# Stores, loads and buffers moved around the seams of a fused attention and two-MoE kernel

## The chip, the cores and the metric

The kernel runs on one core of a Trainium2 chip. TensorE multiplies matrices into PSUM banks; ScalarE, VectorE and GpSimd work on the results in SBUF; SyncE issues the DMA transfers, one after the other, and each of its instructions waits for what it needs before the next one is looked at. The metric is the device time of one execution in microseconds; lower is better. In the profile PE, ACT, DVE, POOL and SP are TensorE, ScalarE, VectorE, GpSimd and SyncE.

## What is computed

Attention of 4 x 8 heads over 576 tokens of width 64, its local part mixed with a read from a memory, then two gated layers over all 2304 tokens of width 512 with a hidden width of 1536. The weight matrices come as float64 words; the kernel turns them into float32 itself.

```python
def _attn_ref(q, k, v, M_prev, z_prev, beta):
    scores = scale * np.matmul(q, k.transpose(0, 1, 3, 2))
    ...
    local = np.matmul(a, v)
    ...
    return (g * mem_out + (1 - g) * local).astype(np.float32)

def _moe_ref(x, w_gate, w_val, w_out):
    gate = 1.0 / (1.0 + np.exp(-(x @ w_gate)))
    val = x @ w_val
    return (gate * val @ w_out).astype(np.float32)

def _moe2_ref(x, w_gate, w_val, w_out):
    g = x @ w_gate
    silu = g * (1.0 / (1.0 + np.exp(-g)))
    val = x @ w_val
    return (silu * val @ w_out).astype(np.float32)
```

## The kernel before

Every operand of a matmul is split into a rounded high part and a low rest, and a product is three passes (high x high, high x low, low x high). The program runs through six stretches.

*Attention* (to about 366 us). Its order is made by due times in a table. Beside it, part of the first layer's weights is converted from words, and values `x @ w_val` for the first tokens are computed ahead and stored to DRAM (`vs`).

*Last values* (`values`, 367 to 392 us). Twelve chunks of 12 matmuls for 384 tokens. ScalarE copies each bank to a buffer `vo`, of which there are two, and SyncE stores it to `vs`. At the same time `right(j)` prepares token block j = 0 and 2 for the blocks: it loads rows `xraw` of `xs` (four tiles, two for each half k), builds seven sums on VectorE and casts them on ScalarE to `xop`. Up to here a scheduler sets the order.

*First blocks* (`blocks`, 392 to 581 us). From here on the order is as written. A weight matrix is cut in six groups p of 256 hidden columns; a run (s, j) multiplies group p of the gate (s = 0) or value matrix (s = 1) with token block j (2 x 384 tokens) by seven products instead of eight, each of six matmuls (L828). In group 0 the runs are run 0 = (0, 0), run 1 = (0, 2), run 2 = (1, 2), run 3 = (0, 1); later groups have (0, 0), (0, 1), (0, 2), (1, 2), so run 5 is (0, 1) of group 1. Only for j = 2 are values computed; for j = 0 and 1 they are known and are loaded from `vs` (`vi`, two tiles of a run, in four buffers). Each product has a number n, seven for a run; the work behind a product is put down for a later number (`later`) and done in `slot(n)`: `keep` copies a bank to c (ScalarE, L874), `add` adds a bank to c (VectorE, L877), `finish` makes one of four quarters of h (ScalarE L837, VectorE L839 or L841). When both quarters of a half f are done, `finish` has SyncE store that half to `hs` (L845) at once: halves f = 1 and f = 0 of a run that starts at n are complete in slots n + 10 and n + 13. h tiles are taken two at a time when a run with s = 0 begins, from five buffers (six in the second layer). Other work is put into slots by `put(at, steps, first, last)`: `right(1)` (rows loaded in slots 0 and 13, used from slots 6 and 15), the seven weight operands of the next half group (`kept` loads the kept weights `ws` into a `raw` buffer, two of which exist; for group 1's values in slot 31, used from slot 37), and conversions of output weights.

*First down projection* (`outputs(0)`, 582 to 738 us). 72 steps (t, m): four or three matmul chains of one tile t of 384 tokens with chunk m of the hidden width, 12 matmuls (L974). `hidden` loads a tile of `hs` to `hd`, casts it on ScalarE (L956) and subtracts on VectorE (L957), two steps ahead; `pairs[i]` loads two chunks of converted output weights into a `raw` buffer and splits them, `words` loads and converts the last two chunks from their words. The result `yb` stays in SBUF, the last third goes to `xs` in DRAM.

*Second blocks* (740 to 1002 us) and *second down projection* (`outputs(1)`, to the end) do the same for the second layer with Silu, six runs in a group and no known values. In both layers the first four loads of `hd` (`prelude`) stand in the last slots of the blocks; in the second layer they take c buffers, each of which comes free with the last operation on its c.

## Time and profile before

| | us |
|---|---|
| three runs | 1150.32, 1154.95, 1156.98 |
| median | 1154.95 |
| the profiled execution, own time | 1159.61 |
| its span, first to last instruction | 1157.8 |
| PE busy / DVE busy / ACT busy | 1111.7 / 805.5 / 599.9 |

Busy time is an average over the six stretches. In the blocks and down projections TensorE runs on end and rarely stops, so each stop is read by itself: the timeline of PE shows it in brackets with its length and the instruction that ended it, and the timelines of the other engines show what that instruction waited for. The granted clock (PEclk) is a share of 2.4 GHz.

### The profile page before, as it was taken

Reading aid. Unit: us, or ns where it says so; the run is one execution under the profiler, and the core shown is the slowest. Engines: PE = TensorE matmul, PEld = TensorE weight load, DVE = VectorE, ACT = ScalarE, POOL = GpSimd, SP = SyncE. Lnnn points to the kernel's source line nnn. Section 1 sums busy time; section 2 is a strip of 40 time slices with the busy share of each in tenths; the row PEclk is TensorE's granted clock in tenths of the full one; section 3 lists DMA queues with packets and bytes.
Section 4 is the critical chain, followed back from the end, with each engine's and each line's share of the span. In section 5 each row is a group of like instructions: output and inputs, shape, how many; then the busy total and the mean of one; then the engine's idle time right before and its main releaser. Section 6 shows DMA issues by size and latency. Waiting matters only on the chain.

```text
span 1157.8 us, 19120 instructions
## 1 busy us (share of the span) xinstructions
PE 1111.7 (96%) x6416; PEld 1004.8 (87%) x6416; DVE 805.5 (70%) x2020; ACT 599.9 (52%) x1470; POOL 164.2 (14%) x209
## 2 busy tenths in 40 slices
PE   7899999998999888999999999999999999899998
PEld 5577877776877888999989999999999999788887
DVE  7898868678767777788865644687877877553332
ACT  5666765575567755555544433555445445332222
POOL 3675542344331000000000000000000000000000
PEclk9888999799799999999999999999999999999999
DMA  5566537445411556666775333334444443554443
GB/s 135 173 185 178 157 98 221 118 128 168 150 55 56 191 173 209 224 223 226 241 239 163 93 95 108 104 107 130 143 147 120 154 134 131 183 168 126 126 123 103
DMA packets 162356, 173.77 MB, mean 150 GB/s; under 512 B 69329, under 2 KB 127697, under 8 KB 162257
## 3 DMA queue, kind: packets, MB, share of 16 engines
q1 hardware_dynamic: 162112, 172.54, 48.3%
q8 instruction: 51, 0.84, 0.3%
q14 instruction: 49, 0.39, 0.1%
q10 hardware_dynamic: 144, 0.00, 0.0%
HBM read 112.20 MB, written 60.29 MB: 149 GB/s over the span
## 4 chain that ended last, share of the span: by engine, by line
PE 76%; DMA 6%; DVE 5%; ACT 2%; issue 1%; SPq 0%; ACTq 0%; DVEq 0%
PE ps L828 34%; PE ps L971 13%; PE ps L974 11%; PE gv L742 6%; PE sc L316 3%; PE av L396 3%; DMA xraw<-xs 2%; PE tp L363 2%; PE sc L302 1%; DMA hd<-hs 1%; PE av L387 1%; DMA raw<-ws 1%; DMA raw<-in_moe_w_gate_dram 1%; PE tp L254 1%; PE tp L355 1%
## 5 line engine op out<-in xcount | busy, mean ns | idle before, releaser
L828 PE MATMUL ps<-xop,wset 128*128 128x384 f32 x2520 | 445.6, 337 | 12.3 <-ACT c L874 12.3
L828 PEld LDWEIGHTS ps<-xop,wset 128*128 128x128 f32 x2520 | 441.2, 188 | 15.7 <-ACT c L874 15.5
L957 DVE TENSOR_TENSOR hl<-hd,hl 128x384 fp32r<-128x384 f32 x144 | 80.3, 558 | 151.8 <-ACT hl L956 150.8
L956 ACT CAST hl<-hd 128x384 fp32r<-128x384 f32 x144 | 74.0, 514 | 189.0 <-PE ps L971 84.7
L874 ACT COPY c<-ps 128x384 f32<-128x384 f32 x180 | 86.0, 479 | 116.4 <-PE ps L828 115.5
L742 PE MATMUL gv<-x,w 128*128 128x256 f32 (+2 forms) x720 | 131.3, 327 | 3.5 <-ACT vo L31 1.7
L877 DVE TENSOR_TENSOR c<-ps,c 128x384 f32<-128x384 f32 x180 | 99.6, 554 | 43.6 <-ACT c L874 20.2
L742 PEld LDWEIGHTS gv<-x,w 128*128 128x128 f32 x720 | 112.4, 202 | 13.0 <-issue 6.8
L974 PE MATMUL ps<-hl,xop 128*128 128x384 f32 x648 | 114.0, 336 | 0.0
L974 PEld LDWEIGHTS ps<-hl,xop 128*128 128x128 f32 x648 | 112.6, 188 | 0.0
L971 PE MATMUL ps<-xop,hl 128*128 128x512 f32 x486 | 111.9, 391 | 0.0
L971 PEld LDWEIGHTS ps<-xop,hl 128*128 128x128 f32 x486 | 91.9, 189 | 19.3
L338 POOL TENSOR_SCALAR s<-s,sum,omg 128x512 f32<-128x512 f32 (+2 forms) x92 | 72.5, 799 | 111.1 <-DVE sum L334 19.7
L837 ACT ACTIVATE h<-c 128x384 f32<-128x384 f32 x108 | 56.7, 525 | 58.0 <-DVE c L877 57.8
L330 ACT ACTIVATE s<-s,nm 128x256 f32<-128x256 f32 (+3 forms) x128 | 71.8, 563 | 15.6 <-DVE nm L319 14.5
L316 PE MATMUL sc<-qka 64*128 64x384 f32 (+3 forms) x384 | 74.8, 386 | 4.5 <-DVE nm L319 2.2
L319 DVE CUSTOM_DVE_ANT_0 s<-sc,mask 128x256 f32<-128x256 f32 (+3 forms) x128 | 59.7, 485 | 17.1 <-PE tp L355 8.9
L316 PEld LDWEIGHTS sc<-qka 64*128 64x128 f32 x384 | 48.6, 211 | 20.8 <-issue 5.1
L500 ACT ACTIVATE a<-raw 128x512 f32<-128x512 f32 x72 | 48.4, 673 | 33.7 <-DMA raw<-in_moe_w_gate_dram 19.5
L31 ACT COPY p<-tp 128x512 f32<-128x512 f32 x96 | 45.0, 494 | 25.4 <-PE av L396 12.5
L507 DVE SCALAR_TENSOR_TENSOR a<-raw,a 128x512 int32<-128x512 int32 x72 | 53.3, 740 | 0.2
L511 DVE SCALAR_TENSOR_TENSOR a<-raw,a 128x512 int32<-128x512 int32 x72 | 50.3, 698 | 0.3
(143 smaller groups left out, 1482.9 us busy)
## 6 DMA issues: line engine op xcount, KB each, us to landing
hs<-h SPq DMA_DIRECT2D x72, 384.0 KB, 2.6
hd<-hs SPq DMA_DIRECT2D x144, 192.0 KB, 2.5
raw<-in_moe_w_val_dram SPq DMA_DIRECT2D x24, 512.0 KB, 4.2
raw<-in_moe_w_gate_dram SPq DMA_DIRECT2D x24, 512.0 KB, 4.4
raw<-in_moe_w_out_dram SPq DMA_DIRECT2D x24, 512.0 KB, 3.9
ws<-a SPq DMA_DIRECT2D x44, 256.0 KB, 2.4
vi<-vs SPq DMA_DIRECT2D x24, 384.0 KB, 4.2
xraw<-xs SPq DMA_DIRECT2D x16, 384.0 KB, 3.9
```

The costliest lines, as they stand in the source:

```text
L316: nc.tensor.matmul(o, lhsT=qk[hr, x, 0, qs], rhs=qk[hr, y, 1, 0:n], start=k == 0, stop=k == 2)
L319: nc.vector.tensor_tensor_reduce(out=dsts[h], in0=o, in1=self.mask[:, m0:m0 + n], scale=-scale, scalar=3.0e38, op0=ALU.add, op1=ALU.min, a ...
L330: nc.scalar.activation(out=s, in_=s, func=ACTF.Exp, bias=nm[:, h:h + 1], scale=-1.0, accum_out=sm[:, h:h + 1])
L338: self.two(f"n{i}", u).tensor_scalar(s, s, r[:, h:h + 1], w, op0=ALU.mult, op1=ALU.mult)
L742: nc.tensor.matmul(o, lhsT=w[:, i, k, :], rhs=x[:, j, k, :], start=n == 0, stop=n == 3 * self.KD - 1)
L828: self.nc.tensor.matmul(o, lhsT=w[:, a, i, k], rhs=x[:, b, j, k], start=first and n == 0, stop=n == 5, skip_group_check=True)
L874: nc.scalar.copy(r.c[n], r.banks[0])
L877: nc.vector.tensor_add(r.c[n], r.banks[bank], r.c[n])
L956: nc.scalar.copy(hl[:, 0], h)
L957: nc.vector.tensor_sub(hl[:, 1], h, hl[:, 0].bitcast(F32))
L971: nc.tensor.matmul(y, lhsT=h[:, i, 128 * c:128 * c + 128], rhs=w[:, j].rearrange("p k f -> p (k f)"), **st)
L974: nc.tensor.matmul(y[:, 0:T], lhsT=w[:, i, c, :], rhs=h[:, j, :], **st)
```

## The change

It has six parts. (1) `finish` returns the store of h, and `blocks` puts it three products later; h tiles are taken by `finish` at their first write, one half at a time. (2) `from_dram(1)` puts the rows of the first half k = 0 into `raw` buffers, and the rows of k = 1 are loaded in slot 6 instead of 13. (3) For the last values, `_Turns` hands out the buffers of converted words (`a`, three) and the two `vo` in turn. (4) In the first seam the third pair of output weights is loaded in the last slots of the blocks, chunks are split one step earlier, and the last two chunks' words are loaded and converted one step earlier; in the second down projection the first of these is loaded one step later. (5) A small activation with Silu is put at step 62 of the first down projection. (6) Two h tiles are taken and not used before the first down projection.

```diff
@@ from_dram @@
-    def from_dram(self, j):
+    def from_dram(self, j, words=()):
...
             for c in range(2):
-                r.append(self.scr.tile([128, 2, T], F32, tag="scr", name="xraw"))
+                if k in words:
+                    t = self.W.raw.tile([128, self.W.n, 2], I32, tag="raw", name="raw").bitcast(F32)
+                    r.append(t.rearrange("p f t -> p (f t)")[:, 0:2 * T].rearrange("p (j t) -> p j t", j=2))
+                else:
+                    r.append(self.scr.tile([128, 2, T], F32, tag="scr", name="xraw"))
                 self.nc.sync.dma_start(out=r[c].rearrange("p j t -> p (j t)"), in_=self.xs[k + 2 * c, :, a:a + 2 * T])
...
@@ finish @@
+        if r.h[f] is None:
+            r.h[f] = self.hp.tile([128, 2, self.T], F32, tag="h", name="h")
         h = r.h[f][:, t]
...
         if (r.s or r.known) and {2 * f, 2 * f + 1} <= r.done:
-            nc.sync.dma_start(out=self.hs[2 * r.p + f, :, a:a + 2 * self.T], in_=r.h[f].rearrange("p t n -> p (t n)"))
+            return lambda: nc.sync.dma_start(out=self.hs[2 * r.p + f, :, a:a + 2 * self.T],
+                                             in_=r.h[f].rearrange("p t n -> p (t n)"))
@@ begin @@
         if r.s == 0:
-            r.h = [self.hp.tile([128, 2, self.T], F32, tag="h", name="h") for _ in range(2)]
-            self.H[r.l, r.p, r.j] = r.h
+            r.h = self.H[r.l, r.p, r.j] = [None, None]
@@ blocks @@
+        def finish(n, r, q, src):
+
+            store = self.finish(r, q, src(r))
+            if store:
+                later(n + 3, store)
...
-                later(n + 3, lambda r: self.finish(r, 0, r.c[0]), r)
+                later(n + 3, finish, n + 3, r, 0, lambda r: r.c[0])
...
-                later(n + 3, lambda r: self.finish(r, 2, r.banks[0]), old)
+                later(n + 3, finish, n + 3, old, 2, lambda r: r.banks[0])
...
-        for n in sorted(set(todo) | set(at)):
-            slot(n)
+        while todo or at:
+            slot(min(set(todo) | set(at)))
@@ run, before the last values @@
+            self.vo = _Turns(self.vo, W, T)
             self.values(*self.fill)
@@ run, first blocks @@
-            steps = self.right(self.from_dram(1), 1, xo[2])
+            steps = self.right(self.from_dram(1, (0,)), 1, xo[2])
             for half, a, b in ((steps[:8], 6, 12), (steps[8:], 15, 21)):
-                put(at, half[:1], a - 6 if a < 15 else a - 2, a)
+                put(at, half[:1], a - 6 if a < 15 else a - 9, a)
                 put(at, half[1:], a, b)
...
             put(at, [pairs[1][0]], b + 24, b)
+            put(at, [pairs[2][0]], b + 27, b)
             self.prelude(at, b + 21, (0, 1, 6, 6), (5, 6))
@@ run, first down projection @@
-                    put(at, [pairs[m // 2][1 + m % 2]], m - 2, 0)
-                for i in range(2, 5):
-                    put(at, [pairs[i][0]], 2 * i - 5 if i > 2 else 0, 0)
-                put(at, [words[0][0]], 5, 0)
-                put(at, words[0][1], 7, 9)
-                put(at, [words[1][0]], 7, 0)
-                put(at, words[1][1], 9, 10)
+                    put(at, [pairs[m // 2][1 + m % 2]], max(m - 3, 0), 0)
+                put(at, [pairs[3][0]], 1, 0)
+                put(at, [pairs[4][0]], 3, 0)
+                put(at, [words[0][0]], 4, 0)
+                put(at, words[0][1], 6, 8)
+                put(at, [words[1][0]], 6, 0)
+                put(at, words[1][1], 8, 10)
...
+                def table():
+
+                    t = self.sums.tile([128, 2, T], F32, tag="s", name="tab")
+                    nc.vector.memset(t[:, 0, 0:2], 0.0)
+                    nc.scalar.activation(out=t[:, 0, 0:1], in_=t[:, 0, 1:2], func=ACTF.Silu)
+
+                put(at, [table], 62, 0)
+
+                for _ in range(2):
+                    self.hp.tile([128, 2, T], F32, tag="h", name="skip")
@@ run, second down projection @@
-                put(at, [words[0][0]], 2, 0)
-                put(at, words[0][1], 5, 8)
+                put(at, [words[0][0]], 3, 0)
+                put(at, words[0][1], 6, 8)
@@ new class @@
+class _Turns:
+    def __init__(self, own, weights, n):
+        self.own, self.weights, self.n, self.k = own, weights, n, 0
+
+    def tile(self, shape, dt, tag, name):
+        self.k += 1
+        return self.weights.number()[:, 0:self.n] if self.k % 2 else self.own.tile(shape, dt, tag=tag, name=name)
```

The other calls of `finish` (quarters 1 and 3) change in the same way.

SyncE's queue, from the last rows of block 2 to the first blocks' slot 16. `vs<-vo` and `vs<-a` are stores of values, `xraw<-xs` and `raw<-xs` token rows, `vi<-vs` values of a run, `hs<-h` stores of h, `raw<-ws` kept weights. Before:

```order
L816 DMA xraw<-xs 128x768
L747 DMA vs<-vo 128x384 x7
L855 DMA vi<-vs 128x768 x2
L747 DMA vs<-vo 128x384
L816 DMA xraw<-xs 128x768 x2
L845 DMA hs<-h 128x768 x2
L816 DMA xraw<-xs 128x768 x2
L855 DMA vi<-vs 128x768 x2
L595 DMA raw<-ws 128x4x128 x2
```

After:

```order
L747 DMA vs<-vo 128x384
L747 DMA vs<-a 128x384
L747 DMA vs<-vo 128x384
L747 DMA vs<-a 128x384
L863 DMA vi<-vs 128x768 x2
L747 DMA vs<-vo 128x384
L821 DMA raw<-xs 128x768 x2
L821 DMA xraw<-xs 128x768 x2
L852 DMA hs<-h 128x768
L863 DMA vi<-vs 128x768 x2
L852 DMA hs<-h 128x768
L595 DMA raw<-ws 128x4x128 x2
```

All four loads of block 1's rows now stand ahead of the first store of h, and the second store of h (run 0, f = 0) stands behind the values of run 3.

ScalarE's queue at the end of the last values; `c<-ps` is the copy of the blocks' first bank. Before:

```order
L31 COPY vo<-gv 128x384 x2
L31 CAST xop<-xsum 128x384
L31 CAST xop<-xraw 128x384 x2
L31 COPY vo<-gv 128x384
L31 CAST wset<-wsum 128x256
L31 COPY vo<-gv 128x384
L31 CAST wset<-wsum 128x256
L874 COPY c_5441<-ps 128x384
L31 CAST wset<-raw 128x256
L31 CAST wset<-wsum 128x256
L837 ACT_TABLE_LOAD
L837 ACTIVATE h<-c_5441 128x384
```

After:

```order
L31 COPY vo<-gv 128x384
L31 CAST xop<-xsum 128x384
L31 COPY a<-gv 128x384
L31 CAST xop<-xraw 128x384 x2
L31 COPY vo<-gv 128x384
L31 CAST wset<-wsum 128x256
L881 COPY c_5439<-ps 128x384
L31 CAST wset<-wsum 128x256
L31 CAST wset<-raw 128x256
L31 CAST wset<-wsum 128x256
L844 ACT_TABLE_LOAD
L844 ACTIVATE h<-c_5439 128x384
```

The copies of the values lie between other casts, and the first bank's copy has one weight cast less ahead of it; the table load keeps its place.

SyncE's queue at the end of the second blocks; `hd<-hs` are the first reads of h for the down projection. Before:

```order
L845 DMA hs<-h 128x768
L582 DMA raw<-ws 128x2x512
L845 DMA hs<-h 128x768
L951 DMA hd<-hs 128x384
L845 DMA hs<-h 128x768
L951 DMA hd<-hs 128x384
L845 DMA hs<-h 128x768 x2
L951 DMA hd<-hs 128x384 x3
L582 DMA raw<-ws 128x2x512
```

After:

```order
L852 DMA hs<-h 128x768
L964 DMA hd<-hs 128x384
L852 DMA hs<-h 128x768
L964 DMA hd<-hs 128x384
L852 DMA hs<-h 128x768 x2
L964 DMA hd<-hs 128x384 x2
L852 DMA hs<-h 128x768
L964 DMA hd<-hs 128x384
L582 DMA raw<-ws 128x2x512
```

The first read has one store less ahead of it, and the third and fourth reads have come ahead of the last store.

## Rows read from the trace of the kernel before

**Rows 1.** The page: busy time of TensorE; ScalarE's busy tenths in 40 slices.

```profile
PE 1111.7 (96%) x6416; PEld 1004.8 (87%) x6416; DVE 805.5 (70%) x2020; ACT 599.9 (52%) x1470; POOL 164.2 (14%) x209
...
ACT  5666765575567755555544433555445445332222
```

**Rows 2.** Windows: stretch, length, busy (x count) of each engine, clock, DMA.

```profile
core 0: us, PE busy (x) PEld busy (x) DVE busy (x) ACT busy (x) POOL busy (x), PEclk, DMA share, GB/s
390.00:400.00 10.00, 7.03 (x39) 6.39 (x37) 7.59 (x19) 7.75 (x18) 0.00 (x0) 1.00 0.61 196
440.00:450.00 10.00, 7.08 (x34) 6.75 (x33) 7.95 (x19) 4.13 (x11) 0.00 (x0) 0.86 0.58 195
...
1010.00:1020.00 10.00, 10.00 (x38) 8.09 (x37) 6.02 (x12) 4.82 (x10) 0.00 (x0) 0.83 0.77 252
```

**Rows 3.** Timeline of PE: start, length, instructions, [idle before <-releaser].

```profile
396.62 2.38 PE L828 MATMUL ps<-xop,wset 128*128 128x384 f32 x12 [1.97 <-ACT c L874]
400.22 7.58 PE L828 MATMUL ps<-xop,wset 128*128 128x384 f32 x42 [1.21 <-ACT c L874]
408.38 7.58 PE L828 MATMUL ps<-xop,wset 128*128 128x384 f32 x42 [0.58 <-ACT c L874]
417.64 3.44 PE L828 MATMUL ps<-xop,wset 128*128 128x384 f32 x18 [1.69 <-ACT c L874]
421.74 22.58 PE L828 MATMUL ps<-xop,wset 128*128 128x384 f32 x126 [0.65 <-ACT c L874]
447.24 13.07 PE L828 MATMUL ps<-xop,wset 128*128 128x384 f32 x65 [2.92 <-ACT c L874]
...
606.23 2.74 PE L974 MATMUL ps<-hl,wset 128*128 128x384 f32 x12 [0.90 <-ACT wset L31]
...
740.66 4.60 PE L828 MATMUL ps<-xop,wset 128*128 128x384 f32 x25 [1.53 <-ACT c L874]
...
1002.19 4.52 PE L971 MATMUL ps<-wset,hl 128*128 128x512 f32 x18 [0.37 <-ACT hl L956]
1009.08 3.39 PE L971 MATMUL ps<-wset,hl 128*128 128x512 f32 x9 [2.37 <-ACT hl L956]
```

**Rows 4.** Timeline of ACT at the first blocks' start.

```profile
392.11 1.03 ACT L31 COPY vo<-gv 128x384 f32<-128x384 f32 x2 [1.17 <-DMA vs<-vo]
...
397.98 1.28 ACT L837 ACT_TABLE_LOAD   x1 [0.78 <-DVE c L877]
...
399.70 0.46 ACT L874 COPY c<-ps 128x384 f32<-128x384 f32 x1
```

**Rows 5.** Timeline of SP in the first blocks; SPq rows are DMA issues.

```profile
407.75 3.81 SPq L845 DMA_DIRECT2D hs<-h  x2
...
433.52 1.94 SPq L855 DMA_DIRECT2D vi<-vs  x2
435.51 0.42 SPq L845 DMA_DIRECT2D hs<-h  x1
436.02 1.62 SPq L595 DMA_DIRECT2D raw<-ws  x2
```

**Rows 6.** Timeline of DVE in the first blocks: its two long waits.

```profile
415.40 0.56 DVE L784 TENSOR_TENSOR xsum<-xraw 128x384 f32<-128x384 f32 x1 [3.72 <-DMA xraw<-xs]
...
441.76 0.43 DVE L633 TENSOR_TENSOR wsum<-raw 128x256 f32<-128x256 f32 x1 [3.84 <-DMA raw<-ws]
```

**Rows 7.** Chain of waits in the first down projection: start, length, what.

```profile
593.97 4.51 DMA raw<-in_moe_w_out_dram
```

**Rows 8.** Timeline of ACT at the second blocks' start.

```profile
738.12 1.28 ACT L837 ACT_TABLE_LOAD   x1 [0.80 <-DMA xs<-yb]
```

**Rows 9.** Chain of waits at the end of the second blocks.

```profile
996.34 1.03 DVE h L841 x2
...
997.77 3.83 DMA hd<-hs
...
1005.64 2.85 DMA hd<-hs
```

**Rows 10.** Stores of h from 405 to 450 us, the tile's own view.

```profile
DMA to landing us min/median/max: 2.3/2.6/5.0
```

More of the change, by code (lines that the diff above doesn't have):

```diff
@@ L913, in blocks @@
                 later(n + 5, add, old, 1, 2)
-                later(n + 6, lambda r: self.finish(r, 1, r.c[1]), old)
+                later(n + 6, finish, n + 6, old, 1, lambda r: r.c[1])
             slot(n + 4)
@@ L922, in blocks @@
                 later(n + 8, add, r, 2, 2)
-                later(n + 9, lambda r: self.finish(r, 3, r.c[2]), r)
+                later(n + 9, finish, n + 9, r, 3, lambda r: r.c[2])
             slot(n + 6)
-        for n in sorted(set(todo) | set(at)):
-            slot(n)
+        while todo or at:
+            slot(min(set(todo) | set(at)))
     @contextmanager
```

## The prediction

> **What bounds the kernel now.** I read the page first: TensorE is busy 96% of the span [rows 1], so a change that leaves every matmul as it is can give back only time in which TensorE stands still or runs at half clock. The windows come next; the reader is to see in them where PE is under its stretch, and what the clock did [rows 2]. Then the timeline of PE alone: each bracket is one gap and its releaser [rows 3]. The ten gaps there sum to 1.97 + 1.21 + 0.58 + 1.69 + 0.65 + 2.92 + 0.90 + 1.53 + 0.37 + 2.37 = 14.2 us. Behind the 2.92 us gap the granted clock is 0.86 over 10 us, behind the 2.37 us gap 0.83: some time at 1.2 GHz instead of 2.4, worth 10 x 0.14 = 1.4 us and 10 x 0.17 = 1.7 us. In the window that holds the gaps of 1.97 and 1.21 us it is 1.00 [rows 2]. So 17.3 us is the ceiling. For each gap I then read the engine that released it, and there whom that engine waited for. The order of instructions of the attention part is the same in both kernels, and so is TensorE's whole order.
>
> The sum is made against the profiled execution, 1159.61 us (span 1157.8). It lies 4.7 us above the median of the three runs, 1154.95 us; I take the gain over to that median.
>
> **Part by part.** One product of the blocks takes 7.58 / 7 = 1.08 us [rows 3]; I call that a slot.
>
> *Five buffers for the last values* (gaps 1.97 and 1.21). With two buffers ScalarE waits 1.17 us for a value store to land before it can copy the next bank [rows 4], and SyncE, which issues everything in order, holds loads of token rows behind those stores. The copy of the blocks' first bank stands behind all this. The change alternates the two buffers with the three of converted words, so that wait goes; three more stores now stand ahead of the second token load, at some 0.4 us of SyncE each [rows 5] about 1.2 us, while the two loads after it no longer wait for ScalarE and come earlier by about as much. VectorE's chain of sums behind these loads is then the late one. The first bank's copy also moves ahead of one weight cast (0.4 us). For the first gap I get between 0.8 us and all of 1.97. The second gap stays whatever the first does: its copy stands behind the table load of 1.28 us, which waits for VectorE's addition [rows 4], and the table load isn't moved here. It may even grow to 1.6 us, since TensorE arrives earlier. Together the bounds are 0.4 and 1.9 us; I take **1.3**, nearer to the upper end because the 1.17 us wait is a row.
>
> *Second tokens' rows at once* (gaps 0.58, 1.69, 0.65). The second pair of row loads stands behind two h stores; SyncE sits on them from 407.75 for 3.81 us [rows 5], because the second store waits for a VectorE product, and VectorE then waits 3.72 us for the rows [rows 6]. That is the 1.69 us gap and most of the 0.65. The change issues all four loads together ahead of any store, seven slots earlier, some 7.5 us where 3.72 were short: the wait goes. What is late next is VectorE's own work in those seven slots, 12 operations for the rows and some 6 for the products, of 0.56 us [rows 6] and overlapping a little, 9 to 10 us against 7.5 us: up to 2 us of lag, while TensorE can run about two slots ahead. So 1.0 to 2.3 us, taken as **1.9**. The first pair of rows now lies in raw buffers of the weights, and its second load must wait until VectorE has read the last raw weights; it gains less than the rest: 0 to 0.58, taken as **0.5**.
>
> *h stored three products later.* In the regular groups of 28 slots no gap is on record to be won; the stores only leave SyncE's way. Two places are touched. The gap of 2.92 us at 447: VectorE waits 3.84 us for kept weights [rows 6], whose load is issued at 436.02 behind a pair of value loads that SyncE holds from 433.52 to 435.46 [rows 5] because their buffers are still being read. That pair isn't moved, one store stands between pair and weights before and after (another one), so the weights land as late as now: **0**. The change adds a wait there: h is now taken from its pool at the first write, and the first h of run 5 needs the buffer of the store that now stands behind that same pair. By its landing of up to 5.0 us [rows 10] ScalarE would stand until about 440.3 with two bank copies queued behind it, and TensorE half a microsecond later, but that lies inside the stretch that the weights set; if the cover fails, it costs 0.5. Bounds -0.5 and 0.
>
> *Words of the first seam* (gap 0.90). The last two output weights arrive late: the chain has a load of 4.51 us from 593.97 [rows 7], which waited for a raw buffer. The pairs ahead of it are loaded and split one product of this stage earlier (12 matmuls of 22.58 / 126 = 0.18 us, 2.15 us [rows 3]), so the buffer comes free 1.3 to 2.2 us earlier and the 0.90 closes: **0.9**. The third pair, a load as large as the one in rows 7, now stands ahead of two reads of h and puts them off by up to 2 us; should TensorE have to wait for them, 0.3 is left, my lower bound.
>
> *Table moved* (gap 1.53). The table load takes 1.28 us between the wait for a store of the last tokens and the first h [rows 8], with the bank copy behind it. At product 62 of the stage before (slice 25 of the page) ScalarE is 3 tenths busy [rows 1], so 0.7 x 2.15 = 1.5 us of each product are idle and cover it; with the cover gone it would cost 1.28 us there. What is late next is the store that the first h still waits for, just ahead of 738.12: TensorE would go on at 740.66 - 1.28 = 739.38, and it is ready at 739.13. **1.3**, bounds 0.9 and 1.5.
>
> The row shows 1.28 us for the load. The Trainium skill (ScalarE: Activation LUTs, What ACT_TABLE_LOAD costs) counts a drain of about 1.38 us with each switch, 2.66 us in all. No row here shows it; if the 0.80 us idle ahead of the load were that drain, the gap would close wholly, 1.53 us in place of 1.3, and the total below would be 10.0 in place of 9.8.
>
> *Second seam* (gaps 0.37 and 2.37, and the clock). Now the first read of h is issued at 997.77 behind a store that waits for a later product, though its own buffer is free with the first operation of the pair at 996.34, and the third at 1005.64 behind the very last store [rows 9]. With stores three products later both go ahead. First read: 0.8 us earlier in the queue, and 384 KB less ahead of it. The split of its data, behind which VectorE's last products of h stand, comes 1 to 2 us earlier, the second read 0.5 to 1 us, and the last product of h, which frees the third read's buffer and ends at about 1005.2 now, ends 1 to 1.7 us earlier: 1003.5 to 1004.2. Third read at about 1003.6, 2.85 us to landing [rows 9], then the cast of 0.5: 1007.0. TensorE, ready at 1009.08 - 2.37 - 0.37 = 1006.34, waits some 0.5 to 0.7 us. Of 2.74 us some 0.5 is left, a gain of 2.2. A gap that short left the clock at 1.00 elsewhere, so the 1.7 us come back as well: 2.2 + 1.7 = **3.9**. Lower bound 0.9: the third read's issue alone, and the clock falls all the same. Upper 4.4.
>
> Sum: 1.3 + 0.5 + 1.9 + 0 + 0.9 + 1.3 + 3.9 = **9.8 us**. The profiled time would be 1149.8 us, the median 1154.95 - 9.8 = **1145.2 us**, 0.85% faster.
>
> **The rivals.**
> *Another wait takes the place.* VectorE's chain sets the first seam (0.4 in place of 1.3, 0 in place of 0.5), and the second seam keeps its fall of the clock (0.9 in place of 3.9). For it: VectorE is the releaser behind the table load [rows 4], and gaps of 2.37 and 2.92 us both cost clock. Against it: the waits named are loads and stores. 9.8 - 0.9 - 0.5 - 3.0 = 5.4 us: 1149.6 us.
>
> *The 447 gap goes too.* If the late weights hang on stores after all, and not on the pair of value loads, 2.92 and 1.4 us come back: 1140.8 us. Against it: the SyncE rows in front of the weights.
>
> *Slower: the five h buffers run out.* In the first stage a store at slot 37 of a group frees the buffer that is written at slot 45. That is 8 slots, 8.7 us, less a landing of 2.3 to 5.0 us [rows 10]: 3.7 us to spare at worst. If SyncE held such a store for more than that and some 2 slots of TensorE's lead, nearly 6 us, each of five groups would have a gap of about 2.5 us and the clock behind it, 5 x (2.5 + 1.7) = 21 us; 1154.95 + 21 - 9.8 = 1166 us. Against it: the longest hold in rows 5 is 3.81 us, and it is one that goes.
>
> *It doesn't do what it says.* The stores' waits move to the loads that now come first, and the gaps come back within the same stage: 1 us, 1154 us.
>
> **How the numbers follow.** The forecast has 0.56, the first rival 0.24, the 447 rival 0.10, the slower one 0.05, no effect 0.05. About 0.5%, 5.8 us, is what a measurement of this kernel can tell from no change. Below 1149.2 us lie the forecast, the 447 rival and nearly half of the first rival: 0.77. Within: the rest of it and no effect, 0.18. Slower: 0.05. The lower bounds sum to 0.4 + 0 + 1.0 - 0.5 + 0.3 + 0.9 + 0.9 = 3.0 us, 1152 us; the upper ones to 11.6 us, 1143.4 us; with most of the 447 rival the range is 1140 to 1152.5 us.
>
> **What would show it.** Right: no PE gap over 0.5 us near 408 to 422; no wait of ScalarE on value stores; PE without a gap near 605; no table load between the two layers' seam and a PE gap of about 0.3 us there; a gap under 1 us after the second product of the last stage and clock 1.00 behind it; and still a gap of nearly 3 us some 50 us into the blocks. Wrong: a gap in the regular groups with ScalarE waiting for a store; the last stage's gap still over 2 us; a larger gap at the table load of the first layer.

## The result, and the profile after

| | before | after |
|---|---|---|
| runs beside the first profile, median (lowest to highest) | 1152.63 us (1146.81 to 1156.98, 4 runs) | 1140.76 us (1132.54 to 1145.86, 4 runs) |
| their ratio, 95% interval | | 0.9878 (0.9838 to 0.9918) |
| later runs, median (lowest to highest) | 1155.64 us (1143.76 to 1160.33, 17 runs) | 1143.24 us (1134.90 to 1149.06, 12 runs) |
| their ratio, 95% interval | | 0.9901 (0.9868 to 0.9934) |
| profiled execution: own time, span | 1159.61, 1157.8 us | 1140.78, 1139.0 us |

The change makes the kernel about 1.0 to 1.2% faster. Forecast was 9.8 us; the medians differ by 11.9 and 12.4 us, the two profiled executions by 18.8 us. To see where they come from, TensorE's timeline after the change is laid beside [rows 3] (start, length, instructions, idle time before and its releaser):

```profile
391.34 2.38 PE L833 MATMUL ps<-xop,wset 128*128 128x384 f32 x12 [0.77 <-ACT c L881]
395.40 40.45 PE L833 MATMUL ps<-xop,wset 128*128 128x384 f32 x228 [1.68 <-ACT c L881]
438.22 130.12 PE L833 MATMUL ps<-xop,wset 128*128 128x384 f32 x744 [2.36 <-ACT c L881]
568.96 2.38 PE L833 MATMUL ps<-xop,wset 128*128 128x384 f32 x12 [0.62 <-ACT c L881]
724.18 2.38 PE L833 MATMUL ps<-xop,wset 128*128 128x384 f32 x12 [0.56 <-ACT c L881]
726.94 258.21 PE L833 MATMUL ps<-xop,wset 128*128 128x384 f32 x1476 [0.38 <-ACT c L881]
985.72 2.38 PE L833 MATMUL ps<-xop,wset 128*128 128x384 f32 x12 [0.57 <-ACT c L881]
```

The gaps of 0.58, 1.69, 0.65, 0.90, 0.37 and 2.37 us are gone, those of 1.97, 2.92 and 1.53 us are shorter, that of 1.21 us is longer, and three stops of 0.56 to 0.62 us, which every run has at the seams, stay. These rows cut the program into stages with the same matmuls in the same order. The first blocks begin where the first gap begins (396.62 - 1.97 = 394.65 before, 391.34 - 0.77 = 390.57 after), the others at the rows with 0.62, 0.56 and 0.57 us in the brackets:

| stage, us | before | after | gain |
|---|---|---|---|
| attention and last values, to the first gap | 394.65 | 390.57 | 4.08 |
| first blocks | 184.73 | 178.39 | 6.34 |
| first down projection and its seams | 157.38 | 155.22 | 2.16 |
| second blocks | 262.68 | 261.54 | 1.14 |
| second down projection | 158.36 | 153.28 | 5.08 |

The first row isn't counted as an effect: attention's instructions have the same order in both kernels, the last values take TensorE 25.26 and 25.23 us, and in the runs below the stage took from 379.6 to 390.6 us. So the profiles show a gain of 14.72 us behind it, which I call REST (763.15 us before, 748.43 us after). The clock in the 10 us behind the stops (columns as in [rows 2]):

```profile
438.00:448.00 10.00, 9.78 (x56) 9.66 (x56) 7.53 (x19) 5.87 (x14) 0.00 (x0) 1.00 1.01 323
991.00:1001.00 10.00, 10.00 (x46) 8.06 (x44) 5.74 (x10) 4.99 (x10) 0.00 (x0) 1.00 0.83 273
```

Both are 1.00 where [rows 2] have 0.86 and 0.83. Behind the first of these stops [rows 3] show the first 65 matmuls; the whole row of before is

```profile
447.24 131.51 PE L828 MATMUL ps<-xop,wset 128*128 128x384 f32 x744 [2.92 <-ACT c L874]
```

and the same 744 matmuls take 130.12 us after: 1.39 us by the clock. SyncE in the first blocks after the change, beside [rows 5]; the loads of the second tokens are `raw<-xs` and `xraw<-xs`:

```profile
390.56 3.21 SPq L821 DMA_DIRECT2D raw<-xs  x2
393.82 0.90 SPq L821 DMA_DIRECT2D xraw<-xs  x2
402.35 0.32 SPq L852 DMA_DIRECT2D hs<-h  x1
402.77 3.40 SPq L863 DMA_DIRECT2D vi<-vs  x2
...
424.07 2.29 SPq L863 DMA_DIRECT2D vi<-vs  x2
426.41 0.42 SPq L852 DMA_DIRECT2D hs<-h  x1
426.93 1.40 SPq L595 DMA_DIRECT2D raw<-ws  x2
```

The hold of 3.81 us on the two stores is gone; the pair of value loads ahead of the kept weights is still held (2.29 us from 424.07). And SyncE at the second seam, beside [rows 9]:

```profile
982.12 0.33 SPq L964 DMA_DIRECT2D hd<-hs  x1
...
988.94 0.79 SPq L964 DMA_DIRECT2D hd<-hs  x2
```

The last products of the second blocks run 999.44 - 985.72 = 13.72 us earlier than before. On that scale the first read is issued 997.77 - 982.12 - 13.72 = 1.9 us earlier than in [rows 9], and the third 1005.64 - 988.94 - 13.72 = 3.0 us. No gap is left there.

### The profile page after: what moved, and what is told of

The parts are those of the page before. It is cut to its first block, busy times and chain, and to the rows that moved or that the text cites. A ratio compares the mean times of both kernels' runs of the same rounds, so it can differ in the third digit from the quotient of the medians.

```text
span 1139.0 us, 19114 instructions
## 1 busy us (share of the span) xinstructions
PE 1101.7 (97%) x6416; PEld 999.4 (88%) x6416; DVE 804.7 (71%) x2021; ACT 601.2 (53%) x1471; POOL 164.3 (14%) x209
## 4 chain that ended last, share of the span: by engine, by line
PE 83%; DVE 6%; DMA 5%; ACT 2%; issue 1%; SPq 1%; POOL 1%; ACTq 0%; DVEq 0%; POOLq 0%
PE ps L833 37%; PE ps L987 13%; PE ps L984 13%; PE gv L742 6%; PE sc L316 4%; PE av L396 3%; PE tp L363 2%; DMA raw<-in_moe_w_gate_dram 2%; PE sc L302 1%; PE tp L240 1%; DVE xop L800 1%; PE tp L254 1%; PE av L387 1%; PE tp L355 1%; DMA raw<-in_moe_w_val_dram 1%
```

## The experiments

All but the two timed kernels at the end were run once, so their own times hold attention's chance (some 10 us). They are compared by stage, cut as above:

| run | first blocks | first down | second blocks | second down | REST |
|---|---|---|---|---|---|
| before | 184.73 | 157.38 | 262.68 | 158.36 | 763.15 |
| after | 178.39 | 155.22 | 261.54 | 153.28 | 748.43 |
| after, second profile (e12) | 180.54 | 155.79 | 261.44 | 153.61 | 751.38 |
| e1: stores at once | 179.26 | 155.17 | 261.45 | 157.93 | 753.81 |
| e2: second tokens' rows as before | 179.10 | 155.21 | 261.43 | 153.44 | 749.18 |
| e6: before, with the later stores alone | 180.50 | 157.28 | 262.86 | 153.69 | 754.33 |
| e3: two value buffers | 179.40 | 155.15 | 261.44 | 153.34 | 749.33 |
| e4: first seam's words as before | 178.68 | 158.29 | 261.44 | 153.73 | 752.14 |
| e5: table load as before | 180.83 | 155.65 | 262.78 | 153.57 | 752.83 |
| e10: kept weights three slots later | 179.30 | 155.16 | 261.43 | 153.53 | 749.42 |
| e7: kept weights three slots earlier | 176.23 | 155.15 | 261.42 | 153.18 | 745.98 |
| e13: the same, timed | 176.51 | 156.07 | 261.46 | 153.16 | 747.20 |
| e8: first table load earlier | 181.40 | 155.80 | 261.45 | 153.36 | 752.01 |

Where an edit leaves a stage alone, second blocks repeat within 0.12 us and the others mostly within 0.9 us; the first blocks scatter more, with their gaps near 390 and 438 us.

**The later stores: taken away, and alone.** e1 issues each store at once again; e6 is the kernel before with this part alone.

```diff
-                later(n + 3, store)
+                store()
```

> The changed kernel with each store of h issued at once again (h tiles are still taken at the first write). By REST I mean the time from the end of the blocks' first product to the end of the span: 763.15 us before the change, 748.43 us after it; attention, whose instructions are the same, is left out by it. Theory: of the parts, the later stores carry the second seam alone (5.05 us of the 14.72 us), since the token rows stand ahead of the stores here either way. REST 753.5 us (753 to 754), PE with the gaps of about 0.4 and 2.4 us and the clock at 0.83 behind them in the second seam, none near 415, and about 2.4 us at 438 as after the change. Rival: the later stores also keep the 438 stall from growing (its gap goes back to 2.9 us with 1.5 us of clock); REST 755.5 us.

> The kernel before with one part of the change, h taken at its first write and stored three products later. Theory: this part alone carries the second seam (5.05 us), frees the row loads of k = 1 (most of 3.0 us) and with that the excess of the gap at 447 and its fall of the clock (2.05 us): REST 763.15 - 10.1 = 753.1 us (752.5 to 754.5). Rival: it carries the second seam only, REST 758.1 us.

e1: 753.81 us, near the theory's 753.5, but in part by luck. Its second down projection is 4.65 us longer, where 5.05 were expected. TensorE's rows show the old gap there, with a clock of 0.83 in the 10 us from 990, while the 438 stop didn't grow. The rest is in the first blocks, 0.87 us longer: there the clock fell behind the first stop, of only 1.81 us, and the 12 matmuls behind it took 3.75 us in place of 2.38 (TensorE, and the window at that stop):

```profile
387.40 3.75 PE L833 MATMUL ps<-xop,wset 128*128 128x384 f32 x12 [1.81 <-ACT c L881]
...
434.11 130.12 PE L833 MATMUL ps<-xop,wset 128*128 128x384 f32 x744 [1.99 <-ACT c L881]
...
990.74 3.30 PE L984 MATMUL ps<-wset,hl 128*128 128x512 f32 x9 [2.34 <-ACT hl L969]
```

```profile
386.00:396.00 10.00, 8.30 (x38) 7.79 (x39) 7.22 (x18) 6.74 (x15) 0.00 (x0) 0.83 0.79 264
```

e6: 754.33 us, 8.8 of the 14.7 us from this one part: 4.67 us in the second down projection, 4.23 us in the first blocks. The gaps of 1.69 and 0.65 us went with it, and the stop of 2.92 us became 0.33 + 2.29 us without a fall of the clock (TensorE of e6, to the second blocks):

```profile
395.87 7.56 PE L828 MATMUL ps<-xop,wset 128*128 128x384 f32 x42 [1.22 <-ACT c L876]
404.20 29.91 PE L828 MATMUL ps<-xop,wset 128*128 128x384 f32 x168 [0.77 <-ACT c L876]
434.44 3.41 PE L828 MATMUL ps<-xop,wset 128*128 128x384 f32 x18 [0.33 <-ACT c L876]
440.14 130.10 PE L828 MATMUL ps<-xop,wset 128*128 128x384 f32 x744 [2.29 <-ACT c L876]
```

So the rival "second seam only" is out. The theory's 753.1 us was 1.2 us low: 0.8 us in the first blocks, where the third gap grew to 0.77 us and 0.33 + 2.29 us stayed of the 2.92, and 0.4 us in the second down projection. Part (6) of the change, and the later words of the second down projection in part (4), have no run of their own; e6 has neither, and its second down projection takes 153.69 us, against 153.28 and 153.61 us after the change.

**The second tokens' rows, as before.**

```diff
-            steps = self.right(self.from_dram(1, (0,)), 1, xo[2])
+            steps = self.right(self.from_dram(1), 1, xo[2])
...
-                put(at, half[:1], a - 6 if a < 15 else a - 9, a)
+                put(at, half[:1], a - 6 if a < 15 else a - 2, a)
```

> The changed kernel with the second tokens' rows as before: all four in xraw buffers, those of k = 1 loaded in slot 13. Theory, from the order of SyncE: with stores three products later these loads stand behind one store of h only, not behind the one that waits for a later product, so they are issued in slot 13 without the 3.8 us hold; the gaps of 1.69 and 0.65 us stay closed though this part is undone. REST 748.4 to 749.3 us. Rival (my prediction's bookkeeping, in which the early loads carry this term): the gaps come back, 3.0 us, and the late sums put VectorE behind, so that the gap at 438 grows to 2.9 us and the clock falls behind it, 2.0 us more: REST 753.5 us.

749.18 us: within the theory's bounds, 4.3 us from the rival's number. SyncE issues the second pair at 402.49 behind one store, and VectorE waits 1.49 us for it in place of 3.72, which TensorE's lead covers (SyncE, then VectorE):

```profile
402.07 0.32 SPq L852 DMA_DIRECT2D hs<-h  x1
402.49 1.78 SPq L821 DMA_DIRECT2D xraw<-xs  x2
```

```profile
408.10 0.56 DVE L785 TENSOR_TENSOR xsum<-xraw,xsum 128x384 f32<-128x384 f32 x1 [1.49 <-DMA xraw<-xs]
```

Either edit closes these gaps, the later stores (e2, e6) or the earlier rows (e1). With the stores moved, the earlier rows bring little: without them a new, small stop stands ahead of the one near 438 us. There ScalarE waits for a store of h, the wait that the change adds, 3.39 us in e2 and 3.29 us in e6 against 2.36 us after the change, and TensorE stops 0.43 and 0.33 us (ScalarE, then TensorE of e2):

```profile
432.00 0.52 ACT L844 ACTIVATE h<-c 128x384 f32<-128x384 f32 x1 [3.39 <-DMA hs<-h]
```

```profile
433.33 3.42 PE L833 MATMUL ps<-xop,wset 128*128 128x384 f32 x18 [0.43 <-ACT c L881]
```

In the time of the whole stage (179.10 us, against 178.39 and 180.54 after the change) this can't be told.

**Two buffers for the last values.**

```diff
-            self.vo = _Turns(self.vo, W, T)
```

> The changed kernel with two buffers for the last values instead of five. REST is the time from the end of the blocks' first product to the end of the span: 763.15 us before the change, 748.43 us after it. Theory: the gaps at the start of the blocks go from 0.77 + 1.68 us back to 1.97 + 1.21 us, and nothing later changes: REST 748.43 + 0.74 = 749.2 us (748.9 to 749.5). Rival: the later row loads make VectorE late further on, with a gap of a microsecond or more within the first 30 us of the blocks: REST over 750.2 us.

749.33 us, as expected in sum, but not in its place. TensorE's first gaps:

```profile
389.09 2.38 PE L833 MATMUL ps<-xop,wset 128*128 128x384 f32 x12 [1.72 <-ACT c L881]
392.68 7.58 PE L833 MATMUL ps<-xop,wset 128*128 128x384 f32 x42 [1.21 <-ACT c L881]
401.13 32.86 PE L833 MATMUL ps<-xop,wset 128*128 128x384 f32 x186 [0.87 <-ACT c L881]
```

The third gap, 0.58 us in [rows 3], is back although the rows of the second tokens are loaded as in the changed kernel. With two buffers the three gaps sum to 3.76 us (before), 1.91 + 1.22 + 0.77 = 3.90 us (e6) and 3.80 us (e3). With five they sum to 2.45 us in the first profile after and to 3.01 us in the second (1.31 + 1.70); in the other runs with the changed kernel's code there (e4, e5, e7, e10, e13) to 2.63 to 3.33 us, and only e4 of these has a third gap, of 0.34 us. So the five buffers carry most of this gap too, and are worth some 0.4 to 1.5 us of gaps in all. The time of the whole stage (179.40 us, between the two profiles after) doesn't show it.

**The first seam's words, as before** (the third pair's load leaves the blocks' last slots, the rest is one step later).

```diff
-            put(at, [pairs[2][0]], b + 27, b)
...
-                    put(at, [pairs[m // 2][1 + m % 2]], max(m - 3, 0), 0)
+                    put(at, [pairs[m // 2][1 + m % 2]], m - 2, 0)
```

> The changed kernel with the output weights of the first seam in their old places (third pair, chunks, and words of the last two chunks one step later). Theory: this part carries the 0.90 us gap and the stops under half a microsecond just ahead of it and the slow restarts behind them, 2.19 us by the two traces: REST 748.43 + 2.2 = 750.6 us. Rival: a share of the 2.19 us came from the later stores of h, which leave SyncE and the DMA queue free ahead of the first reads: REST 749.3 to 750 us, with a gap under 0.9 us near 596 us.

752.14 us: the first down projection is 3.1 us longer than after, where 2.2 were expected; both theories were low. Two gaps stand where the kernel before had one:

```profile
584.16 2.75 PE L987 MATMUL ps<-hl,wset 128*128 128x384 f32 x12 [0.93 <-ACT wset L31]
587.79 2.74 PE L987 MATMUL ps<-hl,wset 128*128 128x384 f32 x12 [0.87 <-ACT wset L31]
```

This part is therefore needed for all of the 2.16 us; why its loss costs 0.9 us more than the kernel before had lost there stays open.

**The table load, as before.**

```diff
-                put(at, [table], 62, 0)
```

> The changed kernel without the small Silu activation in the first down projection, so that the table load stands again in front of the first h of the second layer. Theory: the 0.38 us gap of that seam is 1.28 us longer if the load is all that stands there: REST 748.43 + 1.14 = 749.6 us (the difference of the two traces) up to 749.7 us, the gap 1.5 to 1.66 us. Rival: a table load costs more than the 1.28 us of its row (the Trainium skill, ScalarE: Activation LUTs, What ACT_TABLE_LOAD costs, counts 2.66 us with a drain): then the gap would be 3.0 us and REST 751.1 us.

The second blocks take 262.78 us, 1.24 us longer than in the first profile after and 1.34 us than in the second. ScalarE, beside [rows 8], and TensorE at the second layer's start:

```profile
722.38 1.28 ACT L844 ACT_TABLE_LOAD   x1 [0.87 <-DMA xs<-yb]
723.68 0.52 ACT L844 ACTIVATE h<-c 128x384 f32<-128x384 f32 x1
```

```profile
724.92 5.32 PE L833 MATMUL ps<-xop,wset 128*128 128x384 f32 x29 [1.60 <-ACT c L881]
```

The load costs its row, 1.28 us, the activation starts 0.02 us behind it, and the gap is the theory's (1.60 us, where the rival had 3.0). The Trainium skill (ScalarE: Activation LUTs, What ACT_TABLE_LOAD costs) counts a drain besides, 2.66 us in all; the trace doesn't agree, and the measurement decides. Most of the rest of the run's REST (752.83 us) is in the first blocks, whose code is the changed kernel's: a stop of 3.11 us ahead of 433.08, with the clock at 0.83 behind it. The same code gave 2.36 us, and no fall, in the first profile after.

**The stop at 438 us: later, and earlier.** e10 loads the kept weights three slots later, e7 three slots earlier.

```diff
-                    put(at, turning[:1], b + 3, b)
+                    put(at, turning[:1], b + (6 if p == 1 else 3), b)
```

```diff
-                    put(at, turning[:1], b + 3, b)
+                    put(at, turning[:1], b if p == 1 else b + 3, b)
```

> The changed kernel with one load moved: the kept weights of group 1's values are loaded three slots later, behind one more store of h (384 KB). A test of the clock: the gap at 438 us, 2.36 us after the change with 40 us of uninterrupted products ahead of it, should grow by 1.0 us to about 3.3 us. Theory: the length of the stop decides whether the granted clock falls (2.92 and 2.37 + 0.37 us before, with 1.5 us lost behind each): clock about 0.85 in the 10 us behind the gap, REST 748.43 + 1.0 + 1.5 = 750.9 us. Rival: the stops ahead of it decide (before the change there were gaps of 1.69 and 0.65 us in the 30 us ahead, here none): clock 1.00 behind the gap, REST 749.4 us.

> The changed kernel with one load moved the other way: the kept weights of group 1's values are loaded three slots earlier, ahead of the pair of value loads on which SyncE stands from 424.07 to 426.36 us. Theory: that pair, and nothing else, makes the weights late (VectorE waits 3.27 us for them). They land some 4 us earlier, the gap of 2.36 us closes wholly, and the slow restart goes with it: REST 748.43 - 2.47 = 746.0 us. Rival: ScalarE's wait of 2.36 us for a store of h, which ends at 430.76 us and is new with the change, comes out from under its cover: a gap of 0.5 to 1 us remains, REST 746.5 to 747 us. Second rival: the raw buffer is not yet free, SyncE stands on it and the value loads come late instead: no gain, REST 748 us or more.

e10: the gap is 2.91 us, 0.55 more than in the first profile after, and the clock stayed at 1.00; REST 749.42 us, the rival's number. TensorE's row and the window behind it:

```profile
437.25 130.11 PE L833 MATMUL ps<-xop,wset 128*128 128x384 f32 x744 [2.91 <-ACT c L881]
```

```profile
437.00:447.00 10.00, 9.75 (x55) 9.65 (x56) 8.30 (x21) 6.07 (x14) 0.00 (x0) 1.00 0.99 310
```

But the rival's reason falls as well: e5 had no stop in the 40 us ahead of its 3.11 us and the clock fell. The second profile of the changed kernel (below) had it fall behind 2.55 us, and e1 at the blocks' start behind 1.81 us. Neither the stop's length nor the stops ahead of it decide by themselves.

e7: 745.98 us, as the theory had it; e13, a second profile of it, 747.20 us. The weights go out at 410.11, ahead of the pair that is held, and TensorE stands 0.20 us:

```profile
410.11 1.20 SPq L595 DMA_DIRECT2D raw<-ws  x2
413.15 2.30 SPq L863 DMA_DIRECT2D vi<-vs  x2
```

```profile
425.14 130.09 PE L833 MATMUL ps<-xop,wset 128*128 128x384 f32 x744 [0.20 <-ACT c L881]
```

That settles what made the weights late: the held pair of value loads ahead of them. ScalarE's new wait for a store of h, 2.36 us in the profile after, is still 2.40 us here and costs TensorE at most those 0.20 us:

```profile
419.89 0.53 ACT L844 ACTIVATE h<-c 128x384 f32<-128x384 f32 x1 [2.40 <-DMA hs<-h]
```

**The blocks' start: the first table load, and a candidate.** e8 puts a small Sigmoid activation ahead of the last values. e11 has that, e7's edit, the rows as in e2, and the splits of the first value weights moved behind the first bank's copy.

```diff
+            nc.scalar.activation(out=t[:, 0:1], in_=t[:, 1:2], func=ACTF.Sigmoid)
             self.values(*self.fill)
```

```diff
-            for step in self.right(self.from_dram(2), 2, xo[1]) + turning + splits:
+            for step in self.right(self.from_dram(2), 2, xo[1]) + turning:
...
+            put(at, splits, 0, 5)
```

> The changed kernel with a small Sigmoid activation ahead of the last values, where the attention's exponentials are done, so that the first table load of the blocks (1.28 us at 393.17 in the trace after the change) stands in attention's tail and not between a copy and the first h. REST is the time from the end of the blocks' first product to the end of the span: 748.4 us after the change by the first trace; over the runs with unchanged code there the two gaps at the blocks' start come to 2.45 to 3.15 us. Theory: the second gap, 1.68 to 1.71 us in every run of the changed order, is the table load plus the wait behind VectorE's addition, and falls by 1.28 us to about 0.4 us. Rival: the addition, which itself is behind eight operations for weights, becomes the late one and the gap stays above 1 us.

> A candidate that may beat the changed kernel: kept weights loaded three slots earlier, the Sigmoid activation ahead of the last values, the second tokens' rows as before the change (their part gave nothing by itself), and the casts and subtractions of the first value weights put behind the first bank's copy, into slots 0 to 5 of the blocks. Theory: the first bank's copy then has no weight cast ahead of it and the first addition four operations of VectorE less, so that both gaps at the blocks' start fall under 0.5 us, and the gap at 438 us is gone: REST 746.3 - 2.0 = 744.3 us (743.5 to 745). Rival: VectorE, which has the same work to do within the first fourteen slots, is then late for the second tokens' rows or the first value weights, with a gap of half a microsecond or more near slots 7 to 15: REST 745.3 us or more.

e8: the second gap fell to 0.40 us as forecast, and nothing came of it. A third gap of 1.00 us appeared seven products on, so that the three sum to 3.07 us (3.01 us in the second profile after), and the stop near 438 us was 3.33 us with the clock at 0.83:

```profile
391.66 2.38 PE L833 MATMUL ps<-xop,wset 128*128 128x384 f32 x12 [1.67 <-ACT c L881]
394.45 7.56 PE L833 MATMUL ps<-xop,wset 128*128 128x384 f32 x42 [0.40 <-ACT c L881]
403.00 32.88 PE L833 MATMUL ps<-xop,wset 128*128 128x384 f32 x186 [1.00 <-ACT c L881]
439.21 131.56 PE L833 MATMUL ps<-xop,wset 128*128 128x384 f32 x744 [3.33 <-ACT c L881]
```

e11 has no first gap; the first product ends at 392.17 + 4.62 / 2 = 394.48 us (half of its first row), so REST is 1142.1 - 394.48 = 747.6 us, the rival's side: the time came back in smaller gaps behind, 0.77 and 0.39 us in the first 15 us, and 0.76 and 0.51 us where the stop of 438 us had been. Ahead of the 0.76 us ScalarE waits 3.72 us for a store of h, as in e2.

```profile
392.17 4.62 PE L833 MATMUL ps<-xop,wset 128*128 128x384 f32 x24
...
436.59 3.41 PE L833 MATMUL ps<-xop,wset 128*128 128x384 f32 x18 [0.76 <-ACT c L881]
440.51 130.09 PE L833 MATMUL ps<-xop,wset 128*128 128x384 f32 x744 [0.51 <-ACT c L881]
```

What was made earlier at the very start was waited for again further on. The first blocks take 176.75 us (to the row at 571.23 us), against 176.23 and 176.51 us with e7's edit alone: the rest of the candidate brings nothing.

**Timed: the changed kernel again, and with e7's edit.**

> The changed kernel itself once more, beside the candidate of the same call. REST is the time from the end of the blocks' first product to the end of the span, 748.4 us in its first trace. Theory: the stop near 438 us and those at the blocks' start differ from execution to execution (kernels with the same code there had 1.84 to 3.11 us near 438, and the clock fell only behind 3.11 and 3.33 us), all other stages repeat within 0.3 us. REST 748 to 750 us, or 1.5 us more if the clock falls; the ratio to the kernel before 0.985 to 0.992. Rival: the first trace's 2.36 us is what this order always gives: REST 748.4 to 748.8 us.

> The candidate that beat both in one look, timed: the changed kernel with the kept weights of group 1's values loaded three slots earlier. Theory: 2.4 us less than the changed kernel in every execution, and also the clock's fall where that one has it: REST 746 to 747 us, the ratio to the kernel before 0.982 to 0.989 and some 2 to 3 us below the changed kernel's median. Rival: the gain of the one look was attention's chance, the ratio is the changed kernel's.

The changed kernel: ratio 0.9901 (0.9868 to 0.9934), REST 751.38 us in its profile, which is the theory's 748 to 750 us with the fall of the clock on top; the clock is down to 0.83 behind a stop of 2.55 us:

```profile
433.15 131.58 PE L833 MATMUL ps<-xop,wset 128*128 128x384 f32 x744 [2.55 <-ACT c L881]
```

```profile
433.00:443.00 10.00, 9.85 (x47) 9.85 (x48) 7.48 (x18) 5.57 (x13) 0.00 (x0) 0.83 1.02 325
```

The same 744 matmuls take 131.58 us here and 130.12 us in the first profile: 1.46 us by the clock alone. With e7's edit the median is 1134.18 us (1129.92 to 1137.27, 6 runs), the ratio 0.9825 (0.9783 to 0.9867): 1.3 to 2.2% faster than before, and 9 us under the changed kernel. Its two REST values (745.98 and 747.20 us) lie 1.2 to 5.4 us under the two of the changed kernel (748.43 and 751.38 us), 3.3 us on average. The other 6 us or so go with the granted clock of the whole execution: it was 0.984 on average in these six runs and 0.977 in the twelve of the changed kernel, and among the runs of one kernel the time falls by 0.7 to 0.9 us for each 0.001 of it (a straight line through the runs of each of the three kernels). What set the clock higher isn't shown; the fall near 438 us, 1.46 us, which the edit can save, is a small part of it.

## Why the prediction was right or wrong

The direction, the size of a percent and the 1145.2 us were near (1140.76 and 1143.24 us measured, range 1140 to 1152.5), and the forecast's ratio, 1145.2 / 1154.95 = 0.9916, lies within both intervals. That is partly luck: the sum was too small, and terms missed in both directions. REST fell by 14.7 us in the first profile after and by 11.8 us in the second, where 9.8 were forecast, and some terms stood with the wrong part.

| term | forecast (bounds) | measured | what carried it |
|---|---|---|---|
| five value buffers, gaps 1.97 and 1.21 | 1.3 (0.4 to 1.9) | 3.18 - 2.45 = 0.73; 0.17 in the second profile | the buffers (e3) |
| second tokens' rows, gap 0.58 | 0.5 (0 to 0.58) | 0.58 | the buffers, for the most part (e3) |
| the same, gaps 1.69 and 0.65 | 1.9 (1.0 to 2.3) | 2.34, with the slow restarts 3.07 | rows or later stores, either (e1, e2, e6) |
| stop at 447 | 0 (-0.5 to 0) | 0.56, and 1.39 by the clock; in the second profile 0.37 and nothing | kept weights that land earlier; for the clock, open |
| first seam | 0.9 (0.3 to 0.9) | 2.16 | words moved (e4) |
| table | 1.3 (0.9 to 1.5) | 1.14; by e5 1.24 to 1.34 | table (e5) |
| second seam | 3.9 (0.9 to 4.4) | 5.08 | later stores (e1, e6) |

*The step that failed: a stop was priced by its bracket.* The ceiling of 17.3 us was gaps plus clock. But a stop costs more than its bracket. In [rows 3] 12 matmuls take 2.38 us and 42 take 7.58 us: 0.173 us for each more, and 0.30 us for the row besides. Matmuls overlap (the page of before has 337 ns as the mean of one), and at a stop this overlap is lost. So an estimate from these two rows is the bracket and 0.3 us on top. [rows 3] bear it out: 42 + 42 + 18 + 126 = 228 matmuls in 7.58 + 7.58 + 3.44 + 22.58 = 41.18 us of busy rows, and the same 228 in one row of 40.45 us after. That is 0.73 us beside three stops (0.9 by the estimate), which is in the 3.07 us of the table. At the first seam it is larger. There TensorE's rows of before (the next one is in [rows 3]) and of after, over the same place, read:

```profile
600.30 5.03 PE L974 MATMUL ps<-hl,wset 128*128 128x384 f32 x24
```

```profile
589.90 6.47 PE L987 MATMUL ps<-hl,wset 128*128 128x384 f32 x36
```

Before, 24 and 12 matmuls go from 600.30 to 606.23 + 2.74 = 608.97 us, 8.67 us; after, the same 36 take 6.47 us. So 2.20 us were lost where the bracket says 0.90. The other 1.30 us count as busy time: the busy rows are 5.03 + 2.74 = 7.77 us in place of 6.47. I took the closing of this gap right and its worth less than half.

*The value buffers* were put too high: 1.3 us forecast, 0.73 and 0.17 us measured, under the lower bound in the second profile. The wait for value stores went, as forecast, and the second gap grew, as forecast (1.68 us). But the first gap stayed at 0.77 and 1.31 us, as the first bank's copy still stands behind casts, and one of them waits for VectorE's weights (ScalarE after the change, the copy is at 390.82); in e11, with these splits moved, that gap is gone.

```profile
390.50 0.41 ACT L31 CAST wset<-wsum 128x256 fp32r<-128x256 f32 x1 [0.38 <-DVE wsum L633]
```

*The second seam* went as its steps said, only further. The third read was put at 1003.6 us on the old scale; it was issued at 988.94 + 13.72 = 1002.66 us. Its cast (ScalarE) ran at 991.32 without TensorE waiting, so nothing of the 0.5 us that I left there remained: 2.74 us of gaps in place of 2.2, and 5.08 - 2.74 = 2.34 us by clock and slow restarts in place of 1.7.

*The stop at 447* was put at 0, and this step failed as well. That its gap would stay was right (2.36 and 2.55 us), and so was the mechanism, which e7 shows, and the new wait of ScalarE, which came and was hidden. But the weights don't land as late as before: counted from the blocks' first gap, SyncE issues them 5.0 us earlier (436.02 - 394.65 = 41.37 us before, 426.93 - 390.57 = 36.36 us after), TensorE's products come 4.4 us earlier, and VectorE waits 3.27 us for the weights in place of 3.84 (VectorE after the change, beside [rows 6]):

```profile
432.73 0.43 DVE L633 TENSOR_TENSOR wsum<-raw 128x256 f32<-128x256 f32 x1 [3.27 <-DMA raw<-ws]
```

The pair itself is held no less long (2.29 us, 1.94 before). And the clock: before, its fall was taken as part of the stop. At this place it fell behind 2.55, 2.92, 3.11 and 3.33 us, and not behind 2.91 us or those of 2.36 us and less, with stops in the 30 us ahead or without; at the blocks' start it fell behind 1.81 us in e1. So whether 1.39 us are gained there differs between executions of one kernel.

*Which part does what.* I wrote that loading the second tokens' rows at once carries 1.9 us and that the later stores win nothing in the first group. e2 and e6 show that the later stores alone do nearly as well: the second store of h moved behind the row loads frees them by itself, which the order of SyncE's queue shows and I didn't use. The 0.5 us of the first pair belong mostly to the value buffers.

The rivals: "another wait takes the place" came true in part at the blocks' start, where it had 0.4 us in place of 1.3 and 0.17 to 0.73 us were measured, and in e8 and e11; its 0 for the 0.58 us and its second seam are out. The five h buffers held in the changed kernel: ScalarE's one wait for a store of h, 2.36 us, is hidden. The margin is small: in e2, e6 and e11, with the rows late, it is 3.3 to 3.7 us and TensorE stops 0.33 to 0.76 us. The clock rule of the forecast, "a gap that short left the clock at 1.00 elsewhere", wasn't put to the test at the second seam, as no gap was left.

## What to carry to other kernels

Price a stop by what the engine got done over the place, matmuls per microsecond before, in and behind it, and not by the idle time in one bracket. In a queue that issues in order, look for the instruction that is held and move anything that is ready ahead of it: three slots earlier, ahead of the held value loads, the kept weights (e7) brought 1.2 to 5.4 us behind attention, 3.3 us on average. When two edits free the same load, only a run without each tells which is needed, and the gain of a stage is not the sum of its parts.

## What the runs showed that I had not expected

Behind attention the second blocks repeat within 0.12 us (261.42 to 261.54 us in the eleven runs with the moved table load), the down projections mostly within 0.9 us, and the first blocks within 2.5 us where the code is the same, while attention alone differs by 11 us (379.6 to 390.6 us) between executions with the same instructions; most of the scatter of the totals lies there. It goes with the granted clock: over 20 to 370 us this was 0.92 in the longest attention (394.65 us, before), 0.93 after (390.57 us), 0.96 in e12 (384.82 us) and 0.97 in the two shortest (381.36 us in e4, 379.62 us in e7). Which of the two sets the other isn't shown.

In the first blocks and at the second seam the clock fell to 0.83 or 0.86 over 10 us behind stops of 1.81 to 3.33 us, and not behind one of 2.91 us; at the second seam it fell behind 2.34 (e1) and 2.37 us, where in the first blocks 2.36 us left it at 1.00. What decides stays open.
